# Reordering the opening of a fused attention and MLP kernel on one Trainium2 core: warming matmuls, second down scores, first local value sums

## Chip, cores and metric

The kernel runs on one core of one Trainium2 chip. The metric is the device time of one execution in microseconds (us); lower is better. Engines are named as in the profile: PE (TensorE matmul), PEld (TensorE weight load), DVE (VectorE), ACT (ScalarE), POOL (GpSimd), SP (SyncE).

## What is computed

Inputs are q, k, v of shape 8 x 8 x 576 x 64 (batch, head, position, head dimension) and two matrices, w_in (512 x 2048) and w_out (2048 x 512). Cut to what matters:

```python
def sm_attn(qq, kk, vv):                       # "down" attention
    s = scale * qq @ kk.T
    return softmax(s) @ vv
q_d, k_d, v_d = mean of 4 neighbours of q, k, v      # 576 -> 144 positions
out_up = repeat(sm_attn(q_d, k_d, v_d), 4)
mask   = abs(pos_i - pos_j) < 4                      # "local" attention
out_local = softmax(where(mask, scale * q @ k.T, -1e9)) @ v
x = (out_up + out_local) as 4608 x 512
h = x @ w_in
y = (h * sigmoid(1.702 * h)) @ w_out                 # float32, 4608 x 512
```

## The kernel before

**Stages.** The 4608 rows of x are worked through in nine groups of 512 (loop at L1017). For each group, `mm1` (L828, matmuls at L813) multiplies x by w_in and applies the gate on ACT (`silu`, L824); `mm2` (L854, matmuls at L891 and L906) multiplies by w_out and stores. The attention of batch b+1 is woven into the matmuls of group g at fixed step numbers (`POS`, `POS_0`). Only batch 0 has no matmuls to hide under: its attention is an opening of some 22 us, lines L929 to L1015, and all edits lie there. The schedule is manual: each engine executes its instructions in the order in which the lines below issue them, and the framework only adds the semaphores.

**The opening on POOL and DMA.** POOL starts the loads in this order: k and q of head group 0 (L930, `load_1` L218), k and q of head group 1 (L933, L935), five chunks of v into `vb` (`load_vb0`, L260), and then, behind a copy that waits for the second v chunk (`gate`, L941), w_in, the next batch's k and q, and w_out.

**The opening on PE, in order.**

- L949 `warm4(41, 64)`: 164 matmuls of zeros, 64 x 64 weights by 64 columns, on four tile positions in turn (L777). L950 `warm(7)`: seven matmuls of zeros, 128 x 128 by 512 columns (L769). Their results are never read. They write the two PSUM banks `PM`.
- L955, L956 `bars0` (L409): writes a large negative number where the local band is masked. L958 `scores0(0, i)` (L421): local scores of head group 0; needs the transposed k and q that DVE makes (`prep_1`, L312). L959 `exp0(0)` (L483): their exponentials on ACT.
- L966 `warm(4, t=PM[0])`, L967 bars again, L969 `scores_d(0, 0, PB[2])` (L464) and `exp_down(0)` (L499): down scores of head group 0, needing the sums over four neighbours that DVE makes (`reduce_qk`, L331).
- L970 to L974: local scores of head group 1. L975 `exp0(1)`: ACT reads them in the order PM[0], PM[1], PB[2], `most(0)` = PB[0], `most(1)` = PB[1].
- L979, L980 `prep_vd_pe` (L386): the value sums over four neighbours, as matmuls with a 0/1 matrix `psel`. They come in two parts: parts kc 0 and 1 into PM[0] (ten matmuls, v chunks 0 to 3), then part kc 2 into PM[1] (four matmuls, v chunks 3 and 4). DVE copies each part to `vd` (L394).
- L981 `scores_d(0, 1, PB[2])` and `exp_down(1)`: down scores and exponentials of head group 1, 24 matmuls at L464 and one ACT instruction at L499. L982 loads ACT's next table.
- L983 to L986, for each head pair hp of 0 to 3: `av_local0` (ten matmuls, L512: local attention times v), `av_down0` (twelve, L525: down attention times `vd`), and on DVE `normalise0` (a reciprocal at L542, a product at L543). The output bank is `o[hp] = PB[hp % 3]`, so pair 0 uses PB[0], pair 1 PB[1], pair 2 PB[2], pair 3 PB[0] again.
- L1003 onward: `turned(hp)` transposes each pair on PE (L563), ACT copies it to `xT` (L574 to L576), and the first matmuls of `mm1` for group 0 (`part`, L813) are put between.

Two waits by buffers matter to what follows: PB[0], PB[1] and PB[2] are PSUM tiles that ACT's exponentials of L975 read, so the local value matmuls of pair 0 may not start before `most(0)` has ended, those of pair 1 not before `most(1)`, and those of pair 2 not before `exp_down(1)`; and pair 3 may not start before `normalise0` of pair 0 has ended on DVE.

```python
for n, kcs in enumerate(((0, 1), (2,))):
    prep_vd_pe(0, PM[n], kcs, eng=nc.vector)
exp_down(1, scores_d(0, 1, PB[2]))
nc.scalar.preload_act_table_set("silu_and_others")
for hp in range(4):
    av_local0(hp, o[hp], range(5))
    av_down0(hp, o[hp])
    normalise0(o[hp], y[hp])
```

Of the kernel before, what the change touches and what calls it, by code (L numbers as in the profile page):

```python
# [19 lines left out]
def kernel(  # L20
# [9 lines left out]
    nc = tc.nc  # L30
# [44 lines left out]
    PM = [psum.tile([128, 512], FP32, name=f"pm{i}") for i in range(2)]  # L75
# [3 lines left out]
    def pm_tile():  # L79
        turn["m"] += 1  # L80
        return PM[turn["m"] % 2]
# [94 lines left out]
    def make_up():  # L176
        nc.scalar.copy(out=up, in_=id128[:, :, None].to_broadcast([128, 128, 4]))
# [112 lines left out]
    def load_w_out(c):  # L290
        nc.gpsimd.dma_start(
            out=w_out_bf[:, 4 * c : 4 * c + 4, :],
            in_=bass.AP(
                tensor=moe_w_out.tensor, offset=moe_w_out.offset + c * 512 * d_model,
                ap=[[d_model, 128], [128 * d_model, 4], [1, d_model]],
            ),
        )
# [74 lines left out]
    def prep_vd_pe(b, pv, kcs=range(3), eng=None):  # L372
        vb, vd = vbs[b], vds[b]

        def heads(x, j):
            if b == 0:
                return x.rearrange("p (hp j) d -> p hp j d", j=2)[:, :, j]
            return x.rearrange("p (m u j) d -> p m u j d", m=2, u=2)[:, :, j]

        for kc, iis in ((0, (0, 1)), (1, (1, 2, 3)), (2, (3, 4))):  # L380
            if kc not in kcs:
                continue
            c0 = 256 * (kc - kcs[0])
            for i in iis:
                for j in range(2):
                    nc.tensor.matmul(  # L386
                        pv[64 * j : 64 * j + 64, c0 : c0 + D * HP],
                        lhsT=psel[b][i // 4][:, PSEL_AT[i, kc] : PSEL_AT[i, kc] + 64],
                        rhs=heads(vb[:, i, :, 0:D], j),
                        start=(i == iis[0]), stop=(i == iis[-1]),  # L390
                        tile_position=(0, 64 * j),
                    )
        cp = eng.tensor_copy if eng else nc.scalar.copy
        cp(  # L394
            out=vd[:, kcs[0] : kcs[-1] + 1, :, 0:D],
            in_=pv[:, 0 : 256 * len(kcs)].rearrange(
                "p (k h d) -> p k h d", k=len(kcs), h=HP
            ),
        )
# [57 lines left out]
    def scores_d(b, qd, sd=None, rounds=range(6)):  # L457
        bank = [sd[:, u, :] for u in range(2)]
        for n in rounds:
            kc, a = n // 2, n % 2  # L460
            for r in range(4):
                rows = slice(32 * r, 32 * r + 32)
                u, j = (r // 2, r % 2) if b < 1 else (r % 2, r // 2)
                nc.tensor.matmul(  # L464
                    bank[u][64 * j : 64 * j + 64, SD * kc : SD * kc + SD],
                    lhsT=kdT[qd][rows, 48 * kc : 48 * kc + 64, a],
                    rhs=qdT[b, qd][rows, :, a],
                    start=(a == 0), stop=(a == 1),
                    tile_position=(32 * r, 64 * j),
                )  # L470
        return sd
# [26 lines left out]
    def exp_down(qd, sd):  # L498
        nc.scalar.activation(  # L499
            out=eds[qd][:, :, 0:432], in_=sd[:, :, 0:432],  # L500
            func=AF.Exp, scale=inv_sqrt_d / 16.0,
        )
# [6 lines left out]
    def av_local0(hp, o, chunks):  # L509
        for i in chunks:  # L510
            for j in range(2):
                nc.tensor.matmul(  # L512
                    o[:, j, 65 * i : 65 * i + 65],
                    lhsT=ez[hp // 2][:, hp % 2, j, i, :],
                    rhs=vbs[0][:, i, 2 * hp + j, :],
                    start=True, stop=True,
                )

    def av_down0(hp, o):
        Ed, vd, u = eds[hp // 2], vds[0], hp % 2  # L520
        for c in range(2):
            for kc in range(3):
                q0 = SD * kc + 16 * c
                for j in range(2):
                    nc.tensor.matmul(  # L525
                        o[:, j, 65 * (5 + c) : 65 * (6 + c)],
                        lhsT=Ed[64 * j : 64 * j + 48, u, q0 : q0 + 128],
                        rhs=vd[64 * j : 64 * j + 48, kc, hp, :],
                        start=(kc == 0), stop=(kc == 2),
                        tile_position=(64 * j, 0),  # L530
                    )

    def y_tiles0():
        return (
            work.tile([128, 7, 2, D], BF16, name="y", tag="y", bufs=4),
            work.tile([128, 2, 7, 1], FP32, name="rc0", tag="rc0", bufs=4),
        )

    def normalise0(o, y, c0=0, c1=7):
        y, rc = y  # L540
        ov = o[:, :, 0:455].rearrange("p x (c e) -> p x c e", e=65)
        nc.vector.reciprocal(rc[:, :, c0:c1], ov[:, :, c0:c1, 64:65])  # L542
        nc.vector.tensor_tensor(  # L543
            out=y[:, c0:c1].rearrange("p c x d -> p x c d"), in0=ov[:, :, c0:c1, 0:D],
            in1=rc[:, :, c0:c1].to_broadcast([128, 2, c1 - c0, D]), op=ALU.mult,
        )
# [219 lines left out]
    def warm(n, cols=512, t=None):  # L766
        t = pm_tile() if t is None else t
        for _ in range(n):
            nc.tensor.matmul(  # L769
                t[:, 0:cols], lhsT=wz[:, 0:128], rhs=wz[:, 0:cols], start=True, stop=True  # L770
            )

    def warm4(n, cols):
        for _ in range(n):
            for r in range(4):
                u, j = r // 2, r % 2
                nc.tensor.matmul(  # L777
                    PM[u][64 * j : 64 * j + 64, 0:cols],
                    lhsT=wz[64 * u : 64 * u + 64, 0:64], rhs=wz[64 * u : 64 * u + 64, 0:cols],
                    start=True, stop=True,  # L780
                    tile_position=(64 * u, 64 * j),
                )
# [141 lines left out]
    o, y, x = {}, {}, {}  # L924
# [21 lines left out]
        load_qk(1, qd)  # L946
    load_w_out(0)
    load_w_out(1)
    warm4(41, 64)  # L949
    warm(7)  # L950
    make_up()
    make_psel0()
    prep_1("k", 0, 0)
# [22 lines left out]
    for hp in range(4):  # L976
        o[hp] = PB[hp % 3]
        y[hp] = y_tiles0()
    for n, kcs in enumerate(((0, 1), (2,))):  # L979
        prep_vd_pe(0, PM[n], kcs, eng=nc.vector)  # L980
    exp_down(1, scores_d(0, 1, PB[2]))  # L981
    nc.scalar.preload_act_table_set("silu_and_others")  # L982
    for hp in range(4):  # L983
        av_local0(hp, o[hp], range(5))
        av_down0(hp, o[hp])
        normalise0(o[hp], y[hp])  # L986
    make_dm()
# [100 lines left out]
```

## Time and profile before

| | |
|---|---|
| median of 3 runs | 314.51 us (314.37 to 315.09) |
| the profiled execution | 313.9 us, of which 312.1 us is the span of the trace |
| PE busy in the span | 304.5 us (98%) |
| ACT, DVE, POOL busy | 203.2, 148.6, 148.3 us |
| mean granted TensorE clock | 0.995 |

The profile comes from one execution. Times in it are us from the start of the span; the execution's own time is 1.8 us longer than the span. A timeline row reads: start, length, engine, line, operation, output<-input, shape, count, and in brackets the idle time of the engine just before it and what ended it. Several equal instructions in a row are merged (x10), and the length is then from the first start to the last end. Matmuls are pipelined: one takes about 0.2 to 0.3 us from start to end, but the next starts long before that, so what a block costs PE is the time from its start to the start of the next block.

### The profile page before, as it was taken

The page shows a single profiled execution, that of the slowest core. Times are in us where ns is not written, and L with a number is a line of the kernel's source. Part 1 is how long each engine was busy: PE and PEld are TensorE (multiplying, and loading weights), DVE is VectorE, ACT ScalarE, POOL GpSimd, SP SyncE. Part 2 cuts the span into 40 slices and gives each one's busy share as a digit, 9 for nine tenths or more (in the row PEclk, how much of TensorE's full clock was granted, in tenths as well). Part 3 has the DMA queues.
Part 4 walks back from the last instruction along what each step waited for, and adds up shares of the span by engine and source line. Part 5 has one row for each costly group of instructions (what it writes and reads, how often), then busy time and mean ns, then how long its engine had stood idle before and what let it go on. Part 6 is the DMA issues. An engine that isn't in the chain of part 4 may idle for free.

```text
span 312.1 us, 9894 instructions
## 1 busy us (share of the span) xinstructions
PE 304.5 (98%) x4308; PEld 155.4 (50%) x4308; DVE 148.6 (48%) x304; ACT 203.2 (65%) x327; POOL 148.3 (48%) x169
## 2 busy tenths in 40 slices
PE   8799999999999999999999999999999999999995
PEld 4475555454644554455545554555455544444444
DVE  4984946761495059605980399028912760000000
ACT  4475775787867687668866895589558857316611
POOL 8552294294238943795359734982397210000000
PEclk9799999999999999999999999999999999999999
DMA  6999999889527951696159714982330110011011
GB/s 108 135 199 211 186 125 209 216 213 245 143 103 169 216 126 68 169 223 154 52 173 199 186 38 145 203 197 70 122 103 33 40 69 0 34 67 36 0 67 67
DMA packets 64043, 39.95 MB, mean 128 GB/s; under 512 B 44544, under 2 KB 54912, under 8 KB 64000
## 3 DMA queue, kind: packets, MB, share of 16 engines
q0 software_dynamic: 18784, 14.94, 33.5%
q1 hardware_dynamic: 45072, 24.32, 27.5%
q8 instruction: 33, 0.54, 0.8%
q14 instruction: 10, 0.08, 0.1%
q10 hardware_dynamic: 144, 0.07, 0.1%
HBM read 44.81 MB, written 9.44 MB: 174 GB/s over the span
## 4 chain that ended last, share of the span: by engine, by line
PE 92%; DMA 3%; POOL 2%; issue 1%; ACT 1%; DVE 1%; POOLq 0%; DVEq 0%; ACTq 0%
PE pm L891 37%; PE pm L813 25%; PE pa L813 15%; PE pa L437 3%; DMA vb<-in_v_dram 3%; PE pa L891 2%; PE pa L692 2%; PE pa L670 2%; PE pa L464 2%; PE pm L906 1%; POOL vb L260 1%; PE pa L605 1%; PE pa L563 0%; PE pa L593 0%; POOL kb L218 0%
## 5 line engine op out<-in xcount | busy, mean ns | idle before, releaser
L891 PE MATMUL pm<-w_out_bf,gT 128*128 128x512 bf16 x528 | 119.5, 379 | 0.0
L813 PE MATMUL pm<-xT,w_in_bf 128*128 128x512 bf16 (+1 forms) x354 | 88.9, 378 | 0.1
L813 PEld LDWEIGHTS <-w_in_bf 128*128 128x128 bf16 x581 | 56.2, 98 | 65.8 <-issue 0.3
L891 PEld LDWEIGHTS <-gT 128*128 128x128 bf16 x560 | 52.7, 98 | 62.6 <-issue 0.8
L824 ACT ACTIVATE gT<-pm 128x512 bf16<-128x512 f32 x88 | 52.7, 604 | 41.0 <-PE pm L813 41.0
L813 PE MATMUL pa<-xT,w_in_bf 128*128 128x512 bf16 (+1 forms) x227 | 59.0, 376 | 0.0
L507 DVE TENSOR_TENSOR es<-es,mask 128x600 bf16<-128x600 bf16 x28 | 17.5, 662 | 85.8 <-ACT es L475 85.7
L876 ACT ACTIVATE osb<-pm 128x512 f32<-128x512 f32 (+2 forms) x35 | 20.3, 582 | 30.5 <-PE pm L891 28.0
L824 ACT ACTIVATE gT<-pa 128x512 bf16<-128x512 f32 x56 | 32.1, 610 | 6.3 <-PE pa L813 6.3
L762 POOL TENSOR_TENSOR xT<-xT,od 128x576 bf16<-128x576 bf16 x12 | 16.7, 1394 | 38.5 <-DVE xT L746 38.2
L746 DVE TENSOR_TENSOR xT<-n,l 128x285 bf16<-128x285 f32 (+1 forms) x96 | 28.2, 367 | 0.0
L343 POOL TENSOR_TENSOR pq<-kT 128x576 f32<-128x576 bf16 x11 | 12.8, 1159 | 30.4 <-DVE kT L312 30.4
L878 DVE TENSOR_SCALAR osb<-pm 128x128 f32<-128x128 f32 x1 | 0.3, 293 | 53.7 <-ACT osb L876 53.7
L360 POOL TENSOR_TENSOR pq<-v 112x512 f32<-112x512 f32 x18 | 23.7, 1316 | 4.1 <-DMA v<-in_v_dram 4.1
L312 DVE STREAM_TRANSPOSE kT<-kb 128x576 f32<-128x576 f32 x16 | 19.9, 1245 | 4.7 <-DMA kb<-in_k_dram 4.7
L312 DVE STREAM_TRANSPOSE qT<-qb 128x576 f32<-128x576 f32 x16 | 19.8, 1240 | 1.2 <-DMA qb<-in_q_dram 1.1
L499 ACT ACTIVATE ed<-pa 128x864 bf16<-128x864 f32 x16 | 14.3, 895 | 6.8 <-PE pa L464 6.8
L475 ACT ACTIVATE es<-pa 128x600 bf16<-128x600 f32 x28 | 17.2, 670 | 0.1
L741 ACT ACTIVATE l<-l 128x1440 f32<-128x1440 f32 x12 | 16.8, 1403 | 0.4
L736 DVE COPY n<-pa 128x492 f32<-128x492 f32 x24 | 15.0, 665 | 2.3 <-ACT l L735 1.7
L437 PE MATMUL pa<-qT,kT 32*64 32x60 bf16 x1120 | 15.6, 195 | 0.0
L437 PEld LDWEIGHTS <-kT 32*64 32x64 bf16 x1120 | 14.0, 105 | 3.0 <-DVE es L507 3.0
(132 smaller groups left out, 356.0 us busy)
## 6 DMA issues: line engine op xcount, KB each, us to landing
out_dram<-osb SPq DMA_DIRECT2D x34, 256.0 KB, 2.3
vf<-in_v_dram SPq DMA_DIRECT2D x60, 128.0 KB, 4.3
v<-in_v_dram SPq DMA_DIRECT2D x72, 96.0 KB, 3.1
kb<-in_k_dram POOLq DMA_DIRECT2D x16, 288.0 KB, 6.7
qb<-in_q_dram POOLq DMA_DIRECT2D x16, 288.0 KB, 8.7
w_out_bf<-in_moe_w_out_dram POOLq DMA_DIRECT2D x4, 512.0 KB, 13.3
w_in_bf<-in_moe_w_in_dram POOLq DMA_DIRECT2D x2, 512.0 KB, 6.4
w_in_bf<-in_moe_w_in_dram POOLq DMA_DIRECT2D x1, 1024.0 KB, 12.6
```

What stands on the lines that cost most here:

```text
L312: nc.vector.transpose(out=t32.rearrange("p (i c) -> p c i", c=18), in_=store[b, qd].bitcast(FP32).rearrange("p (c d) -> p c d", c=18),)
L360: eng.tensor_tensor(out=t1[0:112], in0=x[:, :, 0:2, :], in1=x[:, :, 2:4, :], op=ALU.add)
L437: nc.tensor.matmul(P[1 + r // 2][64 * par : 64 * par + 64, r % 2, 60 * i : 60 * i + 60], lhsT=kT[b, qd][rows, k0 : k0 + 64, a], rhs=qT[b, ...
L475: nc.scalar.activation(out=es[2 * qd + u][:, :, 0:300], in_=sp[u][:, :, 0:300], func=AF.Exp, scale=inv_sqrt_d,)
L507: nc.vector.tensor_tensor(out=ev, in0=ev, in1=mask, op=ALU.mult)
L741: nc.scalar.activation(out=l, in_=l, func=AF.Exp, scale=-1.0)
L746: nc.vector.tensor_tensor(out=out, in0=sub(n, *part), in1=sub(l, *part), op=ALU.mult)
L762: eng.tensor_tensor(out=xs, in0=xs, in1=sub(od[:, u, :], 0, (1, SD), (0, 4)), op=ALU.add)
L813: nc.tensor.matmul(acc[:, c : c + n], lhsT=w_in_bf[:, dmc, ffc * 128 : (ffc + 1) * 128], rhs=xT[dmc][:, g * TG + c : g * TG + c + n], star ...
L824: nc.scalar.activation(out=gT[:, ffc, :], in_=acc, func=AF.Silu, scale=GELU_SCALE)
L876: eng.activation(out=osb, in_=ap, func=AF.Copy, scale=1.0 / GELU_SCALE)
L891: nc.tensor.matmul(ops[t], lhsT=gT[:, ffc, t * 128 : (t + 1) * 128], rhs=w_out_bf[:, ffc, :], start=(ffc == 0), stop=(ffc == n_ffc - 1),)
```

## The change

Three edits, all in the opening. (1) Of the seven long warming matmuls, six are issued ahead of the 164 small ones and one stays behind them. (2) The down scores of head group 1, with their exponential and the table load, are issued between the two parts of the value sums instead of behind both. (3) The local value matmuls of pairs 0 and 1 are both issued ahead of the down value matmuls of pair 0; pairs 2 and 3 keep their order.

```diff
     load_w_out(0)
     load_w_out(1)
+    warm(6)
     warm4(41, 64)
-    warm(7)
+    warm(1)
     make_up()
@@
-    for n, kcs in enumerate(((0, 1), (2,))):
-        prep_vd_pe(0, PM[n], kcs, eng=nc.vector)
+    prep_vd_pe(0, PM[0], (0, 1), eng=nc.vector)
     exp_down(1, scores_d(0, 1, PB[2]))
     nc.scalar.preload_act_table_set("silu_and_others")
+    prep_vd_pe(0, PM[1], (2,), eng=nc.vector)
+    for hp in range(2):
+        av_local0(hp, o[hp], range(5))
     for hp in range(4):
-        av_local0(hp, o[hp], range(5))
+        if hp > 1:
+            av_local0(hp, o[hp], range(5))
         av_down0(hp, o[hp])
         normalise0(o[hp], y[hp])
```

The instructions are the same in number and kind on every engine. On ACT, DVE, POOL and SP their order is the same too; only PE's order differs.

## Prediction

> **What bounds the kernel now.** I read the page first: PE is busy for 304.5 of 312.1 us. The view of stretches then gives 286.18 us busy of the last 289.78 us (from 22.32 us on), and the waits of PE from 60 us on are an empty list. So behind 22.3 us PE never waits for anything that is loaded, and whatever moves the start of the stream of L813 moves the end by as much. All three edits lie ahead of that point, in an opening in which PE does wait. I then read the chain of waits between 5 and 24 us:
>
> ```profile
> 8.07 8.68 DMA vb<-in_v_dram
> 16.75 0.04 issue
> 16.79 0.30 PE pm L386 x2
> 17.09 0.51 PE pa L464 x24
> 17.60 0.42 PE pa L512 x10
> 18.02 0.31 PE pa L525 x12
> ...
> 18.42 0.26 DVE rc L542
> 18.68 0.02 issue
> 18.70 1.10 DVE y L543
> 19.80 0.04 issue
> 19.84 0.48 PE pa L512 x10
> ```
>
> The opening ends with: the last v chunk lands (16.75); two value-sum matmuls; the second down scores; local values of pair 0; down values of pair 0; its normalisation on DVE; local values of pair 3, which need pair 0's bank back. From there it is PE and ACT without a gap to 22.32. The timeline of the same place gives starts and waits:
>
> ```profile
> 16.79 0.30 PE L386 MATMUL pm<-vb,psel 128*64 128x256 bf16 x2 [0.23 <-DMA vb<-in_v_dram]
> 17.02 0.58 PE L464 MATMUL pa<-qdT,kdT 32*64 32x144 bf16 x24
> 17.54 0.48 PE L512 MATMUL pa<-vb,l 128*128 128x65 bf16 x10
> 17.95 0.36 PE L525 MATMUL pa<-vd,ed 48*128 48x65 bf16 x12
> ```
>
> ```profile
> 16.85 0.98 ACT L483 ACTIVATE l<-pa 128x960 bf16<-128x960 f32 x1
> 17.70 0.91 ACT L499 ACTIVATE ed<-pa 128x864 bf16<-128x864 f32 x1
> ```
>
> The reader is to see two things. PE idles 0.23 us for the v chunk, which edit 2 can fill. And ACT reads PB[1] (`most(1)`, the first row) until 16.85 + 0.98 = 17.83, which is later than the moment at which edit 3 wants that bank.
>
> **Edit 1, the warming.** The 164 small matmuls run from 1.20 to 3.53, 14 ns each; the long ones load weights at 3.93, 4.36, 4.78, 5.21, 5.64, so 0.43 us each. Now: six long ones from 1.20 to 3.78, small ones to 6.11, the last long one to about 6.5, where the seventh ends today. No data hangs on the order (they all read zeros, results are unread). Behind them PE has the bars, done about 7.4, and then nothing until q is transposed:
>
> ```profile
> 8.23 1.25 DVE L312 STREAM_TRANSPOSE qT<-qb 128x576 f32<-128x576 f32 x1 [1.09 <-DMA qb<-in_q_dram]
> 9.54 0.28 PE L421 MATMUL pa<-qT,kT 32*128 32x120 bf16 x2 [2.06 <-DVE qT L312]
> ```
>
> That 2.06 us of idle PE hides the edit; I take 0. What could make it count is the granted clock:
>
> ```profile
> 6.09:9.51 3.42, 1.39 (x10) 0.69 (x9) 2.33 (x3) 0.19 (x1) 3.34 (x6) 1.00 1.00 171
> 9.51:12.92 3.41, 3.38 (x46) 1.82 (x46) 3.41 (x4) 2.53 (x5) 0.00 (x0) 0.50 2.31 155
> 12.92:16.33 3.41, 3.08 (x84) 2.23 (x82) 3.41 (x4) 1.81 (x5) 3.03 (x6) 1.00 1.65 85
> ```
>
> (The columns are length, busy us and count of PE, PEld, DVE, ACT, POOL, then granted clock, DMA.) A stretch with 1.39 of 3.42 us busy is followed by 3.41 us at half clock, and that, with 3.38 busy, by full clock. In the stretch 6.09 to 9.51 the changed kernel has the same bars and the same idle time, so I expect the same slow stretch. [...]
>
> **Edit 2, second down scores ahead of the last value sums.** The first part of the value sums issues its last pair at 16.14 as today. The down scores then wait for DVE's last sum (L331 from 15.13, 1.34 us, so 16.47). A PE start trails an ACT end by 0.05 in this stage (bars at 15.21 behind L499, 14.27 + 0.89 = 15.16); I use that: 16.52. The block costs 17.54 - 17.02 = 0.52, so 17.04. The chunk has landed (16.75), and four value-sum matmuls follow: the last pair costs 17.02 - 16.79 = 0.23, the pair before it 0.11 (16.14 to 16.25 in the trace): 17.38. Today the next block starts at 17.54, so edit 2 alone gains 0.16 us for PE. What is late next is DVE's second copy to `vd`: the last pair starts at 17.15 (17.04 + 0.11), ends 0.30 later, and the copy (1.07 us for both casts less 0.69 for the first, 0.38, to the longer 0.43 by their mean of 0.56) ends at about 17.9. On ACT nothing moves: L499 is behind `most(1)` either way and starts at 17.70.
>
> **Edit 3, local values of pair 1 ahead of down values of pair 0.** Pair 0's local block starts at 17.38 (its bank has been free since about 16.9) and costs 17.95 - 17.54 = 0.41: 17.79. Pair 1's block writes PB[1], which ACT holds to 17.83; with 0.05 it starts at 17.88 (0.09 of waiting), and costs 0.42 (18.24 to 18.66 today): 18.30. Only then comes the down block of pair 0. Behind the waiting matmul everything on PE is queued, and DVE waits for that down block. It starts at 18.30 instead of 17.95: -0.16 + 0.42 + 0.09 = **+0.35 us**. The copy to `vd` (17.9) is hidden under this by 0.4. The normalisation of pair 0 moves from 18.42 to 18.77, its end from 19.80 to 20.15, and with it pair 3's local block (19.84 to 20.19), pair 0's transposes, ACT's copies, and the first L813 (22.32 to 22.67). Pairs 1 and 2 have slack: pair 2's bank is free at 17.70 + 0.91 = 18.61 and wanted at about 18.8. Nothing behind gives the 0.35 back, since it would need PE to wait for a load there.
>
> Bounds of the new wait, which the trace before has not got: nothing if ACT ends earlier (down block at 18.21, +0.26); 0.09 by ACT's rows of today; more by as much as ACT is late in another execution. I take 0.09, as nothing of ACT is touched by the change.
>
> **Sum.** 0 + 0.35 (edits 2 and 3 together): span 312.45, execution 313.9 + 0.35 = 314.25. The median of the three runs is 0.61 above the profiled execution, so for a median I say 314.51 + 0.35 = **314.86 us**, 0.11% slower, which a measurement of this kernel (about 0.2%, 0.63 us) hardly tells from no change.
>
> **Rivals.**
> - *Slower, by a second slow-clock stretch* (0.20). If the share of PE's time that counts in some stretch falls under what keeps the clock, half clock comes in 12.92 to 16.33 or just behind, where PE is on the path. The point from which it decides lies between the 1.39 of 3.42 us that lost the clock and the 3.38 of 3.41 that won it. Price: the L421 block (14.15 to 14.68) takes 0.53 more, the bars and last scores (15.21 to 15.62) some 0.2 more, both in front of `most(1)`; so ACT ends 0.7 later and edit 3 waits for it: 0.35 + 0.7 = +1.05, 315.56. For it: small matmuls now stand last, and their share in what counts is not known. Against: in the profiled execution PE is equally busy in time either way.
> - *No wait at pair 1* (0.12). If q lands earlier, or the clock stays at 1.00 at 9.51, ACT is ahead by half a us. The small matmuls are 328 of PE's first 342 instructions, and one 16 KB instruction load ran at 5.4 us, while q was loading; issuing them later may move that load behind q's landing, up to 0.5 us on DVE's chain. The v chunk at 16.75 still bounds: if the down scores start at 16.25, right behind the first value sums, the last four follow the chunk at once (16.79 + 0.34 = 17.13), local 0 ends at 17.54 and local 1 at 17.96, where the down block starts today. So 0 to +0.26: 314.5 to 314.8.
> - *Faster* (0.18). The median lies 0.61 above the profiled execution, and the highest run 1.19; if that is the clock's slow stretch falling in costlier places, and long matmuls first make it fall better, a median like the profiled one or below results: -0.65, 313.86. A v chunk that lands later than 16.75 helps the same way, but little: today the down block starts 1.20 behind the landing, then 0.04 + 0.23 + 0.41 + 0.42 = 1.10 behind it, so 0.1 us, and only for a landing over 17.2 us (18.30 - 1.10).
> - *Edit 1 does nothing that can be seen* is part of the forecast.
>
> **Numbers.** Forecast (+0.1 to +0.45) 0.50, no wait 0.12, slower 0.20, faster 0.18. The first two are within 0.2%: 0.62. The range takes in the faster case's 313.86 at its edge and the slower case's 315.56: 313.8 to 315.6; what lies beyond either is about 0.2.
>
> **What would show it.** Right: in the changed profile L464 x24 starts near 16.5 without a wait on the v chunk behind it; L512 has a wait on ACT L483 of about 0.1 us at 17.9; L525 starts near 18.30; L542 near 18.77; the first L813 near 22.67; the slow-clock stretch stands once, between 9 and 13 us. Wrong: L525 at or under 17.95; `qT` transposed before 8.2; half clock behind 13 us, or none at all.

## The result, and the profile after

| | before | after |
|---|---|---|
| median | 314.85 us (20 runs, 314.17 to 315.83) | 315.69 us (20 runs, 314.23 to 316.82) |
| ratio after / before | | 1.0024 (95% interval 1.0013 to 1.0034) |
| profiled execution, its span | 313.9, 312.1 us | 315.37, 313.6 us |

The change makes the kernel 0.24% slower, some 0.76 us. A time within 0.2% of the one before was forecast, at +0.35 us. Executions over 1.5% above the fastest of the same kernel are left out of all ratios, counts and means below, and every one of them had a mean granted clock of 0.995 or less. The chain of waits of the changed kernel, at the place that the prediction showed:

```profile
7.20 9.22 DMA vb<-in_v_dram
16.42 0.04 issue
16.46 0.30 PE pm L386 x2
16.77 0.51 PE pa L464 x24
17.28 0.35 PE pm L386 x4
17.62 1.19 PE pa L512 x20
18.82 0.46 PE pa L525 x12
```

The chain still hangs on the load of v, now on its fourth chunk (16.42). The twenty local value matmuls take 1.19 us, where blocks of 0.41 and 0.42 were expected. The timeline has the reasons (start, length, ... and in brackets the idle time before):

```profile
7.05 1.26 DVE L312 STREAM_TRANSPOSE qT<-qb 128x576 f32<-128x576 f32 x1 [0.21 <-DMA qb<-in_q_dram]
15.42 0.31 PE L386 MATMUL pm<-vb,psel 128*64 128x256 bf16 x2 [0.56 <-DMA vb<-in_v_dram]
16.46 0.30 PE L386 MATMUL pm<-vb,psel 128*64 128x256 bf16 x2 [0.73 <-DMA vb<-in_v_dram]
```

q is transposed at 7.05 instead of 8.23, so what hangs on q is some 1.2 us early: the value sums begin at 14.33 instead of 15.62. But the v chunks are not early. The third lands at 15.38 (before: 14.49), the fourth at 16.42 (16.09), the last at 16.81 (16.75), so PE stands still twice, for 0.56 and 0.73 us. Then the granted clock falls; the view of stretches (the first columns are length and PE busy, the third from the end is the clock):

```profile
10.79:14.21 3.42, 2.62 (x72) 1.83 (x71) 3.42 (x4) 1.55 (x5) 0.53 (x2) 1.00 2.49 146
14.21:17.62 3.41, 2.12 (x44) 1.21 (x43) 1.77 (x2) 2.39 (x4) 3.41 (x6) 1.00 1.04 99
17.62:21.03 3.41, 3.31 (x72) 2.97 (x72) 2.02 (x5) 1.88 (x2) 2.17 (x4) 0.50 1.24 206
```

The half-clock stretch stood at 9.51 to 12.92 before, where it cost nothing that can be seen: a second profile of the kernel before, shown below, has no such stretch, and its first L813 starts at 22.45 against 22.32. Now the stretch stands at 17.62 to 21.03, on the path. The first L813 starts at 23.36.

Why is q early? The DMA summaries of two windows, before (4.5 to 10 us) and after (8.5 to 10 us), each hold one load of 16 KB on a queue that the page calls instruction (33 such packets make up 0.54 MB in the kernel before; that they bring PE's instructions, 256 at a time, is worked out below, from the places where PE stops):

```profile
q8 instruction: 1, 0.02, 1.1%
```

```profile
q8 instruction: 1, 0.02, 4.1%
```

Its packet starts at 5.40 before and at 8.96 after. Before, it runs between the loads of k and q, for 0.98 us: 15 of q's 16 parts land by 7.09, the last at 8.21. After, all have landed by 7.03. All 18 profiles of this study agree: where the first load begins at 5.8 or earlier, q is transposed at 7.60 to 8.53, and where it begins at 8.7 or later, at 6.88 to 7.24. The small warming matmuls and their weight loads are 328 of PE's first 342 instructions. They run from 1.20 to 3.53 before and from 3.87 to 5.37 after, and the load begins at 5.40 and at 8.96. I read this as PE asking for the load at a certain place among its instructions.

### The profile page after: what moved, and what is told of

The parts are those of the page before. It is cut to its first block, busy times and chain, and to the rows that moved or that the text cites. A ratio compares the mean times of both kernels' runs of the same rounds, so it can differ in the third digit from the quotient of the medians.

```text
span 313.6 us, 9894 instructions
## 1 busy us (share of the span) xinstructions
PE 303.8 (97%) x4308; PEld 154.6 (49%) x4308; DVE 148.8 (47%) x304; ACT 203.3 (65%) x327; POOL 148.5 (47%) x169
## 4 chain that ended last, share of the span: by engine, by line
PE 92%; DMA 3%; POOL 2%; issue 1%; ACT 1%; DVE 1%; POOLq 0%; DVEq 0%; ACTq 0%
PE pm L891 37%; PE pm L813 25%; PE pa L813 15%; PE pa L437 3%; DMA vb<-in_v_dram 3%; PE pa L891 2%; PE pa L692 2%; PE pa L464 2%; PE pa L670 2%; PE pm L906 1%; POOL vb L260 1%; PE pa L605 1%; PE pa L512 1%; PE pa L563 0%; PE pa L593 0%
## 5 line engine op out<-in xcount | busy, mean ns | idle before, releaser
L891 PE MATMUL pm<-w_out_bf,gT 128*128 128x512 bf16 x528 | 119.4, 379 | 0.0
L813 PE MATMUL pm<-xT,w_in_bf 128*128 128x512 bf16 (+1 forms) x354 | 88.9, 378 | 0.1
L813 PEld LDWEIGHTS <-w_in_bf 128*128 128x128 bf16 x581 | 56.1, 98 | 65.9 <-issue 0.5
L891 PEld LDWEIGHTS <-gT 128*128 128x128 bf16 x560 | 52.7, 98 | 62.5 <-issue 0.6
L813 PE MATMUL pa<-xT,w_in_bf 128*128 128x512 bf16 (+1 forms) x227 | 59.0, 376 | 0.0
L499 ACT ACTIVATE ed<-pa 128x864 bf16<-128x864 f32 x16 | 14.3, 894 | 8.3 <-PE pa L464 8.3
L437 PE MATMUL pa<-qT,kT 32*64 32x60 bf16 x1120 | 15.4, 195 | 0.3 <-issue 0.3
L437 PEld LDWEIGHTS <-kT 32*64 32x64 bf16 x1120 | 13.7, 105 | 3.4 <-DVE es L507 2.5
```

The costliest lines, as they stand in the source:

```text
L437: nc.tensor.matmul(P[1 + r // 2][64 * par : 64 * par + 64, r % 2, 60 * i : 60 * i + 60], lhsT=kT[b, qd][rows, k0 : k0 + 64, a], rhs=qT[b, ...
L813: nc.tensor.matmul(acc[:, c : c + n], lhsT=w_in_bf[:, dmc, ffc * 128 : (ffc + 1) * 128], rhs=xT[dmc][:, g * TG + c : g * TG + c + n], star ...
L891: nc.tensor.matmul(ops[t], lhsT=gT[:, ffc, t * 128 : (t + 1) * 128], rhs=w_out_bf[:, ffc, :], start=(ffc == 0), stop=(ffc == n_ffc - 1),)
```

## Experiments

Each kernel is timed against the kernel before on the same chip. "Half clock" counts the runs with a mean granted clock of 0.995 or less: one 3.41 us stretch at 0.5 in 312 us gives 1 - 0.5 x 3.41 / 312 = 0.9945. Timed beside these experiments, the kernel before has it in 23 of 137 runs, with a mean of 315.81 us, and 314.85 in the others. From one session to the next its share goes from 2 of 31 to 7 of 27.

| kernel | ratio to before (95%) | half clock | q transposed | last v chunk | first L813 |
|---|---|---|---|---|---|
| before (second profile) | 1 | 23 of 137 | 8.12 | 16.88 | 22.45 |
| the change | 1.0024 (1.0013 to 1.0034) | 10 of 20 | 7.05 | 16.81 | 23.36 |
| edit 1 alone | 1.0024 (1.0007 to 1.0042) | 7 of 12 | 6.88 | 16.45 | 22.02 |
| edits 2 and 3 | 0.9992 (0.9978 to 1.0006) | 4 of 12 | 7.87 | 16.66 | 22.12 |
| edit 2 alone | 1.0001 (0.9985 to 1.0017) | 1 of 12 | 8.27 | 16.23 | 22.38 |
| edit 3 alone | 1.0001 (0.9990 to 1.0011) | 1 of 12 | 8.53 | 17.10 | 22.98 |
| 80 small, 6 long, 84 small, 1 long | 0.9993 (0.9978 to 1.0008) | 1 of 12 | 7.78 | 16.71 | 22.28 |
| change + filler ahead of value sums | 1.0036 (1.0014 to 1.0058) | 4 of 12 | 6.96 | 16.70 | 22.54 |
| change + filler in the wait | 1.0027 (1.0008 to 1.0046) | 0 of 12 | 6.90 | 16.30 | 22.45 |
| 108 small, 9 long | 1.0098 (1.0066 to 1.0130) | 1 of 10 | 7.60 | 15.98 | 21.55 |
| 132 small, 8 long | 0.9981 (0.9967 to 0.9994) | 3 of 12 | 8.42 | 16.55 | 22.11 |
| 7 long, 132 small, 1 long | 1.0056 (1.0023 to 1.0089) | 7 of 9 | 7.02 | 17.09 | 23.75 |
| the same + filler in the wait | 0.9981 (0.9963 to 0.9999) | 0 of 12 | 6.98 | 16.73 | 22.65 |
| 40 small, 11 long | 1.0035 (1.0006 to 1.0063) | 4 of 9 | 7.24 | 16.13 | 21.70 |
| 10 long, 40 small, 1 long | 1.0054 (1.0022 to 1.0087) | 5 of 9 | - | - | - |
| 12 long, no small | 0.9951 (0.9932 to 0.9970) | 0 of 9 | 6.98 | 15.81 | 21.38 |
| 12 long, with edits 2 and 3 | 0.9961 (0.9947 to 0.9975) | 1 of 12 | 7.07 | 16.52 | 22.00 |

(The last three columns are single executions. Of 10 long, 40 small, 1 long no profile is compared. Where the text says "before" without more, it means the first profile.)

The last two columns belong together. With the old value order, the first L813 starts 5.56 or 5.57 us behind the last v chunk in eight profiles (both of the kernel before, edit 1 alone, 80-6-84-1, 108-9, 132-8, 40-11 and 12 long): 0.79 to the first local value matmul, 4.78 from there. So it is the last v chunk that sets when the opening ends. With both edits of the value part it is 5.46 and, with 12 long, 5.48, so these two gain 0.1 us. In the profile of 7-132-1, which has a half-clock stretch right behind the last chunk (17.16 to 20.57), it is 6.66: the stretch costs 1.09. In the changed kernel it is 6.55, and its terms can be told apart. From the first local value matmul (17.56) to the first L813 it takes 5.80 us. All five profiles with edit 3 at full clock take 5.09 there, 0.31 more than 4.78, which is the price of pair 1's block ahead of pair 0's down values; the other 0.71 is the half clock. The first local value matmul itself starts where it did before (17.54), as the 0.73 us of waiting for the fourth chunk hold up the down scores.

### Which edit

Edit 1 alone:

```diff
-    warm4(41, 64)
-    warm(7)
+    warm(6)
+    warm4(41, 64)
+    warm(1)
```

> Edit 1 alone (six long warming matmuls, 164 small, one long; the value part as before). Theory A (instruction load): the small matmuls use up PE's first 256 instructions later, so the 16 KB instruction load starts near 9 us instead of 5.4; q lands near 7.0 instead of 8.2, the last two v chunks still land at 16.4 or later, PE waits for them, and the half-clock stretch may fall behind them. Time +0.2 to +0.6 us, most of the change's +0.76. Rival B (order on PE): edit 1 is hidden under PE's wait for q, time within 0.15 us of before.

Edit 1 has the same ratio as the whole change, so it carries the loss as far as the intervals tell. Its profiled execution is not one that shows it: it kept its clock, took 314.87 us and has its first L813 at 22.02. The instruction load starts at 8.75. Its timeline shows the early q and the new wait:

```profile
6.88 1.26 DVE L312 STREAM_TRANSPOSE qT<-qb 128x576 f32<-128x576 f32 x1
```

```profile
15.90 0.42 PE L386 MATMUL pm<-vb,psel 128*64 128x256 bf16 x4 [1.02 <-DMA vb<-in_v_dram]
```

Edits 2 and 3 with the old warming; the diff of the change less that of the warming:

```diff
-    for n, kcs in enumerate(((0, 1), (2,))):
-        prep_vd_pe(0, PM[n], kcs, eng=nc.vector)
+    prep_vd_pe(0, PM[0], (0, 1), eng=nc.vector)
     exp_down(1, scores_d(0, 1, PB[2]))
...
+    prep_vd_pe(0, PM[1], (2,), eng=nc.vector)
+    for hp in range(2):
+        av_local0(hp, o[hp], range(5))
     for hp in range(4):
-        av_local0(hp, o[hp], range(5))
+        if hp > 1:
+            av_local0(hp, o[hp], range(5))
```

> Edits 2 and 3 without edit 1 (warming as before). Theory A: the instruction load stays at 5.4 us, q at 8.2; only the prediction's wait of pair 1 for ACT is left, +0.2 to +0.4 us, L525 near 18.3. Rival B (the order on PE carries the whole change): +0.6 us or more.

Neither is right: 0.9992, no loss at all. Its chain of waits shows why:

```profile
16.17 0.58 PE pa L464 x24
16.75 0.35 PE pm L386 x4
17.09 0.73 PE pa L512 x20
17.82 0.31 PE pa L525 x12
```

The down scores start at 16.17 and the last v chunk lands under them (16.66); the twenty local value matmuls run through without a wait for ACT, whose L499 starts at 16.96 in this execution, not at 17.70. They take 0.73 us, not 0.41 + 0.42. The down block starts at 17.76, 1.10 us behind the v chunk. That is the 1.10 of the prediction's rivals by chance: here the chain comes from DVE's last sum of q and not from the chunk.

Edit 2 alone (`prep_vd_pe` of part kc 2 behind `scores_d(0, 1)`) and edit 3 alone (both `av_local0` ahead of `av_down0(0)`), the lines of `prep_vd_pe` and those of `av_local0` in the diff above:

> Edit 2 alone. By the prediction's sum: the second down scores fill the wait for the last v chunk, pair 0's local block starts 0.16 us earlier, but the down block waits for DVE's copy to vd until about 17.95, so -0.1 to +0.1 us. Rival: the last value sums, now behind the down scores, make the copy and the down block late: +0.2 us or more.

> Edit 3 alone. By the prediction's sum: a block of 0.42 us goes ahead of pair 0's down values; pair 0's local block at 17.54, pair 1's at 17.95 without a wait for ACT (over at 17.83), down block at 18.37: +0.3 to +0.5 us. Rival: DVE's copy to vd or ACT hides the block and the time stays within 0.15 us.

Both 1.0001. For edit 2 that is what was expected, and its profile has the rows of the sum within 0.05 us: down scores at 16.57, value sums at 17.08, local values at 17.43 (16.52, 17.04 and 17.38 in the prediction). Edit 3 was expected at +0.3 to +0.5 us, and its interval ends at +0.35. In its profile both local blocks take 0.73 us, where one took 0.41, and the first L813 starts 5.88 us behind the last v chunk, the 0.31 more than 5.57. So the block does show there, a little smaller than expected; the measured time is too coarse to tell 0.31 from nothing.

### Small ones first, but the same count at the end

```diff
-    warm4(41, 64)
-    warm(7)
+    warm4(20, 64)
+    warm(6)
+    warm4(21, 64)
+    warm(1)
```

> The kernel before with the warming split: 80 small, six long, 84 small, one long; the value part as before. PE's 256th instruction falls at the same time as with edit 1, but small ones stand first. Theory A: instruction load near 9 us, q near 7.0, PE then waits for the last v chunks, time and share of slow-clock runs as with edit 1 (+0.2 to +0.6 us, about half of the runs). Rival B (long ones first): as before, within 0.15 us, 1 run in 5.

The time is as before, as rival B had it, but the run does not decide: the instruction load started at 4.95, not near 9, so q stayed at 7.78, and theory A would have the time as before too. My guess of when the load is asked for was wrong: 80 small ones in front suffice to keep it ahead of q.

### Moving the instruction loads

108 small and nine long, and twelve long alone:

```diff
-    warm4(41, 64)
-    warm(7)
+    warm4(27, 64)
+    warm(9)
```

> The kernel before with 108 small warming matmuls and nine long ones, in the old order (small first), everything else as before: 108 PE instructions fewer ahead of the scores. Theory A (PE's 16 KB instruction loads share the queue of the data): the first load starts behind q's landing, near 9 to 10 us, the second behind the last v chunk; q lands near 7.0, the last v chunk a us earlier than 16.75, first L813 at 21.3 to 21.8, and the stall of PE near 43 us moves or goes: -0.5 to -1.4 us. Rival B (what matters is that long ones stand first, by the clock): within 0.2 us of before, with slow-clock stretches as seldom as before (about 1 run in 5).

The queue that theory A names is not shared: between 4.5 and 10 us the kernel before has its one instruction load on q8 and the other 830 packets, those of q and v among them, on q0. What the profiles show is that the loads run at the same time.

```diff
-    warm4(41, 64)
-    warm(7)
+    warm(12)
```

> The kernel before with twelve long warming matmuls and no small ones. Theory A: the first instruction load comes only near 13 us, with the scores of head group 1, so q lands near 7.0 and the v chunks are delayed by one load instead of two: -0.3 to -1.2 us against before. Rival B (long ones first make the clock drop): slow-clock stretches in half of the runs as with edit 1, time +0.2 to +0.8 us.

Twelve long ones are the best kernel of the study: 313.35 us, 0.49% under before. The first instruction load starts at 14.87, q is early (6.98), the last v chunk is early too (15.81), and the first L813 starts at 21.38. The kernel with 108 small ones also has an early opening (21.55) and yet is 1% slower. Its list of PE's waits names what neither theory had priced:

```profile
PE pa L692 <- issue: 3.5, 5, 1.6
```

"Issue" is time in which PE waits for nothing that the profile shows. PE stops there at its instructions 1217, 2753, 3521, 4545, 5825 and 6593 (counted in the trace): each is a multiple of 256 less 63. The page of the kernel before has 33 instruction loads for 2 x 4308 PE instructions, one for 261. At each of the six stops PE starts again 1.2 to 1.5 us behind the end of the last packet on the instruction queue. I read this as PE running out of instructions at the end of a load, when the next one is late. The stops lie in L437 and L692, blocks of small matmuls: in the kernel before, 40 of L437 with their 40 weight loads take 0.51 us (from 41.51), 12 of L891 with theirs 2.76 us (from 38.81). With 108 fewer instructions ahead, other ends of loads fall into these blocks.

The kernel before, profiled once more:

> The kernel before once more, for a second profile. Theory S: the first profile (313.9 us, 1 us under the median of all runs) was one without the stall at 42 us; a second one has PE stand still for 0.4 to 1.1 us at its 1536th instruction, and a time near 314.9. Rival: no such stall here either, and the opening differs instead.

```profile
42.31 0.24 PE L437 MATMUL pa<-qT,kT 32*64 32x60 bf16 x5
43.40 0.22 PE L437 MATMUL pa<-qT,kT 32*64 32x60 bf16 x3 [0.84 <-issue]
```

Theory S holds. The second execution took 314.94 us. Between those two starts lie 1.09 us, 0.84 of them idle, at instruction 1473 = 1536 - 63. The last load ahead of it began at 40.13 and ended at 41.70 (39.36 to 40.86 in the first profile). In all seven profiles that stop at this instruction PE starts again 1.4 to 1.9 us behind the end of that load. The first profile, on which the prediction was built, was an execution without this stall.

62 instructions fewer (31 matmuls with their weight loads), in both orders: 132 small and 8 long, then 7 long, 132 small and 1 long:

```diff
-    warm4(41, 64)
-    warm(7)
+    warm4(33, 64)
+    warm(8)
```

```diff
-    warm4(41, 64)
-    warm(7)
+    warm(7)
+    warm4(33, 64)
+    warm(1)
```

> The kernel before with 132 small and then eight long warming matmuls: the old order, but every later PE instruction stands 62 places earlier in the program, so that the ends of PE's 256-instruction loads fall elsewhere. Theory S (near 42 us PE runs out of instructions at its 1536th, in the middle of the small score matmuls of batch 1, because the load is late; the kernel before pays it in most executions): the end of that load falls behind the small matmuls, the stall at 42 us goes, -0.3 to -0.8 us. Rival: those stalls are by chance and not by place, within 0.2 us of before.

> The same number of warming matmuls with edit 1's order: seven long, 132 small, one long. If edit 1 costs its time by the late instruction load near 42 us (theory S), that is gone here, and the time is that of the other shifted kernel within 0.25 us or under it, as q lands earlier. If it costs its time by the longer wait for v and the slow clock (theory A), it stays 0.5 to 0.9 us slower than the other shifted kernel, with slow-clock stretches in about half of the runs.

With small ones first the stall at instruction 1473 is gone and the time 0.19% less, which fits the stall, though the warming itself is shorter too. With long ones first the kernel is 0.75% behind its partner, and neither has that stall; so the order costs time without it. The kernel with long ones first has half clock in 7 of 9 runs.

### The clock, and the wait for v

Five zero matmuls ahead of the value sums, in the changed kernel:

```diff
+    warm(5, t=PM[1])
     prep_vd_pe(0, PM[0], (0, 1), eng=nc.vector)
```

> The changed kernel with five more long matmuls of zeros (1.1 us) ahead of the first value sums, where PE waits for v chunks anyway. Theory A with the clock as its price: PE is busy through the wait, slow-clock stretches fall from half of the runs to 1 in 5 or fewer, and the time comes down by 0.2 to 0.5 us against the changed kernel: +0.25 to +0.55 us against before. Rival (the clock is no part of it): the filler delays the value sums by up to 1 us or changes nothing, +0.76 us or more.

Half clock in 4 of 12 and no gain. The profiled execution is one that kept its clock: the sums begin at 15.52 instead of 14.33, and only 0.18 us of the waits for v are left.

```profile
16.35 0.30 PE L386 MATMUL pm<-vb,psel 128*64 128x256 bf16 x2 [0.18 <-DMA vb<-in_v_dram]
```

It also has the longest stall near 43 us among the profiles of this order, 1.2 us idle. What went on in the four runs with half clock is not on record. So seven matmuls of zeros were put behind the value sums of the third v chunk, where the changed kernel waits longest, in two kernels:

```diff
             for i in iis:
+                if b == 0 and kc == 1 and i == 3:
+                    warm(7, t=PM[1])
                 for j in range(2):
```

> The kernel with seven long, 132 small, one long warming matmuls (7 of 9 runs with a slow-clock stretch, +0.56%), and seven more long matmuls of zeros (1.5 us) between the value sums of v chunks 2 and 3, where PE stood still from 14.92 to 16.74 us. Theory A (standing still while v is awaited is what loses the clock): slow-clock stretches in 1 run in 4 or fewer, mean time 1.5 to 2.5 us under that kernel, so within 0.3% of the kernel before. Rival (the clock is lost by something else, the order of the warming or the load itself): half clock in more than half of the runs as without, time no better.

> The changed kernel with the same seven matmuls of zeros at the same place, where its profile shows PE standing still from 15.43 to 16.46 us. Theory A: slow-clock stretches fall from half of the runs to 1 in 4 or fewer; of the +0.76 us about 0.2 to 0.4 goes (the part of the clock), the rest stays. Rival: half clock in half of the runs, +0.76 us or more.

No half clock in either, 0 of 24 runs, against 17 of 29 without the filler. The kernels without filler were not run again on that chip, where the kernel before has half clock in 2 of 22 runs (7 of 27 where the 7 of 9 were measured); a share of the difference may be the chip's. The two views of stretches for the kernel with 7 long, 132 small, 1 long, without and with the filler:

```profile
13.75:17.16 3.41, 1.86 (x35) 1.02 (x23) 1.84 (x3) 2.33 (x5) 3.22 (x6) 1.00 1.23 66
17.16:20.57 3.41, 3.41 (x72) 2.62 (x70) 1.93 (x4) 2.08 (x2) 2.89 (x5) 0.50 1.24 207
```

```profile
13.75:17.16 3.41, 3.00 (x26) 1.48 (x27) 1.60 (x2) 2.10 (x3) 3.35 (x6) 1.00 1.38 82
17.16:20.57 3.41, 3.30 (x104) 2.70 (x100) 2.77 (x6) 2.17 (x2) 2.74 (x5) 1.00 1.24 203
```

With PE busy for 3.00 instead of 1.86 of 3.41 us the clock stays, and the median falls from 317.38 to 314.41. In the changed kernel the half clock goes as well, but the time stays (1.0027). In its profile the filler itself delays the value sums: they resume at 16.27 behind a chunk that landed at 15.92, and the first L813 starts 6.15 us behind the last chunk, where 5.46 would do. So this run does not price the clock.

The two orders with so few instructions that the first load comes behind q in either: 10 long, 40 small and 1 long, then 40 small and 11 long:

```diff
-    warm4(41, 64)
-    warm(7)
+    warm(10)
+    warm4(10, 64)
+    warm(1)
```

```diff
-    warm4(41, 64)
-    warm(7)
+    warm4(10, 64)
+    warm(11)
```

> Ten long warming matmuls, 40 small ones, one long: edit 1's order, but with 102 instead of 342 warming instructions on PE, so that its first instruction load is not asked for before the scores of head group 1. Theory A (the place of the instruction load among q and v is what costs, not the order): q lands near 7.0, the last v chunk at 16.5 or before, slow-clock stretches in at most 1 run in 4, -0.6 to -1.6 us against before, and within 0.3 us of its partner with small ones first. Rival B (long ones first, small ones behind, make the clock drop): slow-clock stretches in half of the runs or more and +0.5 us or more against its partner.

> 40 small warming matmuls, then eleven long ones: the old order with the same 102 instructions. Theory A: as its partner with long ones first, -0.6 to -1.6 us against before, q near 7.0, few slow-clock stretches. Rival B: 0.5 us or more faster than its partner.

The gain expected did not come: the first load now starts at 13.0, among the last v chunks, and both have half clock in about half of the runs, with small ones first too. So the order by itself is not what loses the clock. The intervals of the two overlap. The kernel with small ones first has its first L813 0.6 us early in its profile (21.70), but loses more than that at instruction 1217, near 43 us:

```profile
PE pa L464 <- issue: 1.3, 1, 1.3
```

Finally twelve long ones with edits 2 and 3:

> Twelve long warming matmuls, no small ones, with edits 2 and 3. Edits 2 and 3 alone moved the time by -0.25 to +0.15 us from run to run; with q at 7.0 the wait for ACT of pair 1 is gone (ACT ends its second large exponential near 16.2), so -1.2 to -1.8 us against before, within 0.3 of the kernel with long matmuls alone. Rival (the prediction's +0.35 holds for edits 2 and 3): 0.3 us or more behind that kernel.

0.9961: as fast as without them within the intervals, so edits 2 and 3 cost nothing here either, and bring nothing that the time can tell.

## Why the prediction was wrong

- **Edit 1, the failing step: "That 2.06 us of idle PE hides the edit; I take 0."** PE's time was hidden, but the step counted only matmuls. With the order of the instructions the load of 16 KB on the instruction queue moved too, from 5.40, beside the load of q, to 8.96, beside those of v. Measured alone, edit 1 costs +0.24%, as much as the whole change. The step had to count the loads of the instructions themselves, and it had to ask what PE does when q comes early and v does not.
- **What the edit did.** q came 1.2 us early, which the rival "No wait at pair 1" had seen as possible (up to 0.5). The rival went on that v would still bound, and that holds: at full clock and with the old value order it is 5.57 us from the last chunk to the first L813, whatever the warming. It missed what went with PE standing still for v: half clock in 17 of 29 runs of two kernels that wait there, and in 0 of 24, on another chip, with matmuls of zeros in the wait.
- **"I expect the same slow stretch."** Wrong: half clock went from 23 of 137 runs to 10 of 20 (edit 1 alone: 7 of 12), and, in the profile of the changed kernel, to a place on the path. That is what the slower rival had forecast. In that profile the stretch ahead of the half clock is one in which PE waits for v and is busy for 2.12 of 3.41 us; what small matmuls count for, no run shows. It was priced at +1.05 and the first L813 is 1.04 later in the profiled execution; but the rival's delay lay on ACT ahead of `most(1)`, the measured one on the value matmuls behind it. The 1.04 are 0.71 of half clock, 0.31 of pair 1's block and 0.02 by which the local values start later. That they come so near 1.05 is chance, as is a median 0.84 us up.
- **Edits 2 and 3, +0.35.** Wrong: -0.25 us by the ratio (-0.7 to +0.2). The down block was to start at 18.30 and started at 17.76 in the profile of edits 2 and 3, and three terms make up the 0.54. The down scores started 0.35 earlier, because q did (7.87, not 8.23). The two local blocks took 0.73 together and not 0.83. The 0.09 of waiting for ACT was nothing: it came from one execution with half clock at 9.51, and the second profile, without it, has ACT done with PB[1] at 17.34 instead of 17.83. Edit 3's block cost 0.31 and not 0.42 in the start of L813, and edit 2's rows gained 0.11 and not 0.16 in its own profile.
- **"PE never waits for anything that is loaded" behind 22.3 us.** Wrong in general: it held in the first profile and not in the second, where PE idled 0.84 us for its own instructions. The second execution took 1.04 us more than the first; 0.13 of that lies ahead of the first L813, and of the rest this stall is PE's only wait.
- **What is not settled.** Half clock is only part of the loss: runs at full clock take 315.18 us with edit 1 and 315.44 with the change, against 314.85, and those with half clock 316.03 and 315.80. From the first L813 to the last matmul the four profiles with edit 1's order and count (two of them with filler) have 286.4 to 287.6 us (mean 287.1), six without it 286.0 to 287.0 (mean 286.6). That points to longer stalls for instructions near 42 us: from start to start, PE loses 0.5 to 1.4 us there in the four, 0 to 1.1 in the six. The two ranges overlap, and this is not shown. Nor is what decides the clock: PE busy for 2.12 of 3.41 us was followed by half clock in the changed kernel, while edit 1's profile kept full clock with 2.06 of 3.41 (12.80 to 16.21), so busy time alone does not decide, and no run shows the point between 1.39 and 3.38 that the slower rival took for granted.

## What to carry to other kernels

Reordering matmuls that nothing reads was not free here, where they and their weight loads are 342 of PE's instructions: +0.24% for edit 1 alone. Count PE's instructions (its stops here lie at multiples of 256 less 63), see which loads run beside an instruction load, and try fewer, longer instructions (here twelve long matmuls in place of 171 gave 0.49%). An engine that gets one operand earlier gains nothing if it then stands still for the other: with q 1.2 us earlier PE waited for v for 0.56 and 0.73 us. Look at the granted clock behind such a wait: with it filled by matmuls of zeros, the kernel with 7 long, 132 small, 1 long went from half clock in 7 of 9 runs to 0 of 12, on another chip. Take two profiles of the kernel before: one of them may be the execution without the stall.

## What the runs showed of the hardware

- The kernel before has 33 instruction loads of 16 KB for 2 x 4308 PE instructions, one for 261, and the places where PE stopped for its instructions are multiples of 256 less 63; I read both as loads of 256. Where a load ran beside q's, in the kernel before, q's last part landed at 8.21, and at 7.03 in the changed kernel, where it did not. A load began at 4.6 to 5.7 us where 80 or more small matmuls led, at 8.7 to 9.8 behind six or seven long ones with 132 or more small ones following, at 13.0 to 15.2 with 40 or none; the packet took 0.9 to 2.4 us. PE idled at such edges for 0.84 us in the second profile of the kernel before, and for 3.5 us on L692 alone in the kernel with 108 small ones.
- Matmuls of zeros in a wait for data took half clock from 17 of 29 runs to 0 of 24, on another chip. A half-clock stretch costs by its place: 1.09 us right behind the last v chunk of 7-132-1, 0.71 us behind the first local value matmul of the changed kernel, nothing that can be seen at 9.51 to 12.92.
